# Reordering the transfers that bring in batch 1 in a fused FFT and gated-FFN kernel: row copies regrouped, the rows' load issued ahead of the table copies, the folds from step 19

## The chip, the cores and the metric

The kernel runs on one core of one Trainium2 chip. The metric is the device time of one execution in microseconds, the median of several runs. All times within an execution count from the start of its span, the first instruction of the program.

## What is computed

The reference takes x (8 batches of 3008 rows by 256 features), does a Fourier transform over rows and features and keeps the real part, and sends the 24064 rows that result through a gated feed-forward block:

```python
X = np.fft.fft(x, axis=1)
X = np.fft.fft(X, axis=2)
x = X.real.astype(np.float32).reshape(B * S, D)
gate = 1.0 / (1.0 + np.exp(-(x @ w_gate)))
val = x @ w_val
return (gate * val @ w_out).astype(np.float32)
```

w_gate and w_val are 256 by 1536, w_out is 1536 by 256.

## The kernel before, in words

The feature transform is merged into the gate and value weights when these are loaded (tiles G1, G2 and ge), the row transform is a set of matmuls against tables of cosines and sines, and the symmetry of both is used by folding: rows and features are added to and subtracted from their mirror images before the transform. Everything is float32.

**Steps.** The body is one loop (L1136 on) over steps i = 0, 1, 2, ...; a step handles one block of 128 hidden features of a chunk of up to 252 spectrum rows. There are 12 steps to a chunk (i0 = NFT = 12), three to a group p, six chunks to a batch (per = 72), 576 steps in all. In step i PE does the two halves of the gate and value product (`front_a`, pf<-pk; `front_b`, pf<-qk), and between them a third of the output product of group (i−5)//3 (`back`). ACT starts the next step's accumulator (`seed`, L766: ek times ge), makes copies and sigmoids; DVE forms z and h for step i−1 (L796, L808, L812). From the second chunk on the output product uses 15 products of sums instead of more plain ones: POOL makes these sums (`H_SUMS`, L818, tile sf), seven in steps with i % 3 = 2 and six in steps with i % 3 = 0. PE reads the first two of the six three steps later.

**Lists of side work.** What else has to be done is hung on the steps by hand: `at(i, f)` appends f to step i's list `side`, run at the step's end; `spare` and `gap` hold pieces for ACT and DVE within the step. A piece hung earlier in the code runs earlier in the step. The instructions of each engine run in the order in which this program issues them, and all transfers named below are issued by SP, in order. SP issues a transfer only when the eighth transfer before it has landed (transfers share eight semaphores in turn).

**The weights' stage** (steps 0 to 12). Weights come in pieces (L375), are converted on ACT, DVE and POOL (L382 to L397), and a merge in steps 1 to 8 (`merge`, up to L420) makes 256 columns of G1 and G2 on PE and ACT and issues two transfers of 128 four-byte values into ge (L420). The seeds of steps 6, 8 and 10, made one step ahead, read the ge values that are loaded in steps 4, 6 and 8: the load of the row that the change's title calls the G row's.

**Batch 1.** Batches after 0 go through a DRAM copy with rearranged rows, `xr`:

- `quarter_x(1)` gives 23 copies into xr: three of zeros (L155, L157), two of 128x3x256 (L168) and 18 of 4x32x256 or 4x31x256 (L163), all called row copies here.
- `load_x(1)` (L146) loads xr into the tile x4 in two halves of 1.5 MB. It needs all row copies landed and the weights' use of the same tile ended.
- `fold_ops(1, 2)` gives 24 pieces: two of L496 and six of L492 on POOL, six of L505 (five on DVE, one on POOL), three of L499 to L502, four of L531, three more of L499 to L502 on POOL. `first_folds` (hung on step 16) hangs them on the steps in `slots`.
- `table_rows` (L206) copies six parts of the cosine and sine tables, reversed, into the DRAM tile rtab, 2x32x753 each. `quarter_load` (L247), four calls of four transfers, loads the tables from the input and from rtab into SBUF.
- `quarter_small` (L255, L256, on ACT) picks columns from these tables, `quarter_other` (L262) moves them between partitions, and `ratios` (L272 to L281, on DVE) computes factors from them. Later POOL, DVE and ACT build smaller tables (`quarter_ops`, L292 to L318).
- `e_load(b)` (L683) loads one feature of every row of batch b into x8, seven transfers of 4-byte pieces; POOL folds x8 (`e_fold`, L687 to L690) in step 36.

The stores of a finished chunk (L921, L925) are issued by SP when DVE has transposed it (L912, tile os). The first chunk's 16 stores come in steps 16 and 17.

Of the kernel before, what the change touches and what calls it, by code (L numbers as in the profile page):

```python
# [81 lines left out]
def kernel(  # L82
# [60 lines left out]
    def load_x(b):  # L143
        X[b] = xp.tile([P, 4, NQ, D], F32, name="x4", tag="x4")
        for h in range(0, 4, 2) if b else ():
            nc.sync.dma_start(out=X[b][:, h : h + 2], in_=XR[b][:, h : h + 2])  # L146
# [3 lines left out]
    def quarter_x(b):  # L150

        copy = nc.sync.dma_start
        src = xf[b]
        dst = XR[b] = dram.tile([P, 4, NQ, D], F32, name=f"xr{b}")
        ops = [lambda: copy(out=dst[TB : TB + 1, :, N3], in_=zero[0:1].to_broadcast([1, 4, D]))]  # L155
        for q in (1, 1 + N3):
            ops.append(lambda q=q: copy(out=dst[HP - 1 : HP, :, q], in_=zero[0:1].to_broadcast([1, 4, D])))  # L157

        def run(lo, q, t, step, skip=0, less=0):
            n = TB - skip - less  # L160
            p0 = t // NQ + step * skip
            rows = src[p0 : p0 + n] if step > 0 else src[p0 - n + 1 : p0 + 1]
            copy(out=dst[lo + skip : lo + skip + n, :, q].rearrange("p h d -> h p d"),  # L163
                 in_=rows[:, :, t % NQ].rearrange("p h d -> h p d")[:, ::step])

        for par in range(2):
            lo = par * HP
            ops.append(lambda par=par, lo=lo: copy(out=dst[lo : lo + TB, :, 0:N3], in_=src[0:TB, :, par:NQ:2]))  # L168
            for q in range(N3):
                own = 2 * q + par  # L170
                less = int((par, q) == (0, 1))
                first = int((par, q) == (0, 0))
                ops += [lambda a=a: run(*a) for a in (
                    (lo, N3 + q, M // 2 - own, -1), (lo + TB, q, M // 4 - own, -1, 0, less),
                    (lo + TB, N3 + q, M // 4 + own, 1, first, less))]
        return ops
# [26 lines left out]
    def table_rows(par, q):  # L203

        p0, qq = divmod(M // 4 - 2 * q - par, NQ)
        nc.sync.dma_start(  # L206
            out=rtab[par * TB : (par + 1) * TB, :, q].rearrange("p t k -> t p k"),
            in_=stab[p0 - TB + 1 : p0 + 1, :, qq].rearrange("p t k -> t p k")[:, ::-1])
# [29 lines left out]
    def quarter_src(g, par, t, cols):  # L238
        return (stab[0:TB, t, par:NQ:2, cols], rtab[par * TB : (par + 1) * TB, t, :, cols])[g]

    def quarter_load(t, par):


        for name, cols in (("odd", slice(NE, NE + NO)), ("ev", slice(0, NE))):
            for g, own, lo in TILES:
                if own == par:
                    nc.sync.dma_start(out=TAB[name][lo : lo + TB, t ^ g, :, 0 : cols.stop - cols.start],  # L247
                                      in_=quarter_src(g, par, t, cols))

    def quarter_small(which, part):  # L250

        for g, par, lo in TILES:
            at_ = slice(lo, lo + TB)
            if (g, par) == (which, part):
                nc.scalar.copy(TAB["self"][at_, 0:N3], TAB["ev"][at_, g, :, 0])  # L255
                nc.scalar.copy(TAB["angle"][at_].rearrange("p (t q) -> p t q", t=2),  # L256
                               TAB["odd"][at_, :, :, 0] if g == 0 else TAB["odd"][at_, ::-1, :, 0])
# [6 lines left out]
    def small_ops():  # L264

        vec, sign = nc.vector, TAB["sign"]

        def signs():
            for g, par, lo in TILES:
                nc.gpsimd.memset(sign[lo : lo + TB], (1.0, -1.0)[g])  # L270
        return signs, (
            lambda: vec.reciprocal(TAB["less"], TAB["cos"]),  # L272
            lambda: vec.tensor_tensor(TAB["tan"], TAB["sin"], TAB["less"], op=ALU.mult),
            lambda: vec.tensor_scalar(out=TAB["less"], in0=TAB["tan"], scalar1=-1.0, scalar2=None, op0=ALU.mult),
            lambda: vec.reciprocal(TAB["self"], TAB["self"]),
            lambda: vec.tensor_tensor(TAB["other"], TAB["other"], TAB["self"], op=ALU.mult),
            lambda: vec.tensor_scalar(out=TAB["other"], in0=TAB["other"], scalar1=sign, scalar2=None, op0=ALU.mult),
            lambda: vec.reciprocal(TAB["cy"], TAB["ev"][:, 0, :, 1]),
            lambda: vec.tensor_tensor(TAB["cx"], TAB["ev"][:, 1, :, 1], TAB["cy"], op=ALU.mult),
            lambda: vec.tensor_scalar(out=TAB["cx"], in0=TAB["cx"], scalar1=sign, scalar2=None, op0=ALU.mult),  # L280
            lambda: vec.tensor_scalar(out=TAB["cy"], in0=TAB["cx"], scalar1=-1.0, scalar2=None, op0=ALU.mult))  # L281
# [400 lines left out]
    def e_load(b):  # L682
        nc.sync.dma_start(out=x8[:, b - 1], in_=xf[b, :, :, :, HD : HD + 1])  # L683
# [319 lines left out]
    side, mid, gap, spare = {}, {}, {}, {}  # L1003

    def at(i, *fs):
        side.setdefault(i, []).extend(fs)
# [18 lines left out]
    i0 = NFT  # L1025
    count = 3 * len(groups)
    calm = lambda lo: (i for i in range(lo, count) if 3 <= i % i0 <= 7)
    for i, f in enumerate(quarter_x(1)):
        at(1 + i // 2 if i < 16 else 9 + (i - 16) // 4, f)
    at(i0 + 1, lambda: load_x(1))  # L1030
    for b in range(1, B):
        at(18 + b, lambda b=b: e_load(b))
    at(3 * i0, e_fold)
    later_e = []
    at(3 * i0 + 4, lambda: later_e.extend(e_joint()))
# [5 lines left out]
        at(i - (8 if i == i0 else 11), lambda i=i: e_rows(i))  # L1041

    for i in range(NQ):
        at(11 + i // 3, lambda i=i: table_rows(i % 2, i // 2))
    at(i0 + 1, raw_tables)
    for i in range(4):
        at(14 + i // 2, lambda i=i: quarter_load(i // 2, i % 2))
    signs, ratios = small_ops()
    at(i0, signs)
    for i in range(4):  # L1050
        spare.setdefault(27 + i, []).append(lambda i=i: quarter_small(i // 2, i % 2))
    at(31, quarter_other)
    for i, f in zip((32, 33, 34, 42, 43, 44, 30, 31, 51, 52), ratios, strict=True):
        gap.setdefault(i, []).append(f)

    def first_folds():

        slots = [17, 17, 17, 18, 19, 20, 21, 22, 23, 24, 25, 25, 26, 26, 28, 30, 33, 35, 37, 39, 41, 44, 47, 50]
        for i, f in zip(slots, fold_ops(1, 2), strict=True):
            at(i, f)  # L1060
        for i, f in enumerate(TURN.pop(1)):
            gap[35 + i] = [f]
        swaps, last, first = MORE.pop(1)
        at(41, swaps[1])
        at(52, swaps[0])
        for i, f in enumerate(first):
            gap.setdefault(45 + i, []).append(f)
        for i, f in enumerate(last):
            gap[56 + i] = [f]

    def first_ends():
        one, two = quarter_ends(1, 1), quarter_ends(1, 0)
        for i, f in zip((55, 65, 65, 66, 66, 67, 67, 68, 68, 69, 69, 70, 70, 71, 71, 72, 73, 74, 75, 76),
                        one[0] + two[0] + one[1] + two[1], strict=True):
            gap.setdefault(i, []).append(f)
    at(16, first_folds)
    at(3 * i0 + 14, lambda: seq_start(1))
    for blk in range(2):
# [152 lines left out]
```

## Time and profile before

| what | value |
|---|---|
| median of 3 runs | 1927.27 us (1927.20 to 1927.51) |
| the profiled execution | 1926.32 us, span 1924.5 us |
| granted TensorE clock, mean | 0.997 |
| busy in the span: PE, DVE, ACT, POOL | 1900.8, 1520.1, 1351.8, 1542.9 us |
| L818 sums on POOL | 2392 instructions, 0.55 to 0.60 us each in the mean |
| L492 on POOL | 42 instructions, 1.27 us each |

How to read it: busy time of PE includes the pipelining of matmuls and is close to the span, so it is the gaps that are of interest. The waits say which engine stood for whom; the timeline gives for each instruction its start, duration and the idle time before it with what ended it; the windows give busy time of every engine, the granted clock and the DMA engines' share in a stretch; the chain of waits follows the work that ended last back through what released each step. Of SP the timeline shows how long it took to issue a transfer, not how long the transfer took.

### The profile page before, as it was taken

The numbers are of one execution on the slowest core, as the hardware profiler recorded it, in microseconds if no ns is written. First come the engines' busy times: TensorE is split into PE (matmuls) and PEld (weight loads), VectorE is DVE, ScalarE is ACT, GpSimd is POOL, SyncE is SP. The second block draws the span as 40 slices with busy tenths as digits, with TensorE's granted clock in tenths as the row PEclk, the third lists the DMA queues.
The fourth block names the chain that finished last, engine by engine and source line by source line (L and its number), as shares of the span: only waits on it lengthen the run. The fifth ranks groups of instructions, "written<-read, shape, count | busy, mean of one in ns | idle before, by whom it ended". The sixth has DMA issues, their size and how long they took to land.

```text
span 1924.5 us, 36049 instructions
## 1 busy us (share of the span) xinstructions
PE 1900.8 (99%) x11836; PEld 1758.3 (91%) x11836; DVE 1520.1 (79%) x3368; ACT 1351.8 (70%) x3235; POOL 1542.9 (80%) x2733
## 2 busy tenths in 40 slices
PE   8989999999999999999999999999999999999999
PEld 6669899999999999999999999999999999999998
DVE  7658879887988789797788877888788887976775
ACT  4757777676767677777777777777767777777775
POOL 2359969996999879997799977998789986877770
PEclk9989999999999999999999999999999999999999
DMA  8453231121112120221212112112120120010001
GB/s 312 124 152 19 63 115 54 52 64 56 39 45 71 40 80 19 61 58 31 85 32 62 40 36 88 39 47 48 35 80 14 30 45 15 15 22 20 14 17 30
DMA packets 196661, 109.33 MB, mean 57 GB/s; under 512 B 134791, under 2 KB 187762, under 8 KB 194682
## 3 DMA queue, kind: packets, MB, share of 16 engines
q1 hardware_dynamic: 195896, 106.50, 20.7%
q8 instruction: 95, 1.56, 0.4%
q14 instruction: 92, 0.75, 0.1%
q10 hardware_dynamic: 546, 0.51, 0.1%
q0 software_dynamic: 32, 0.00, 0.0%
HBM read 71.24 MB, written 47.87 MB: 62 GB/s over the span
## 4 chain that ended last, share of the span: by engine, by line
PE 87%; POOL 5%; DMA 3%; DVE 2%; ACT 2%; issue 1%; SPq 0%; POOLq 0%; ACTq 0%; DVEq 0%
PE pf L133 46%; PE po L133 38%; POOL sf L818 3%; PE sum L133 2%; DMA x<-xr 1%; POOL x L492 1%; DMA x<-in_xf_dram 1%; DMA ge<-G 1%; DVE c L902 1%; DVE z L796 0%; POOL x L505 0%; PE ps L133 0%; ACT pf L766 0%; DMA raw<-in_moe_w_val_dram 0%; DVE h L812 0%
## 5 line engine op out<-in xcount | busy, mean ns | idle before, releaser
L818 POOL TENSOR_TENSOR sf<-h,sf 128x168 f32<-128x168 f32 (+1 forms) x1104 | 619.5, 581 | 77.8 <-DVE h L812 75.4
L818 POOL TENSOR_TENSOR sf<-h 128x168 f32<-128x168 f32 (+1 forms) x920 | 520.7, 585 | 160.5 <-DVE h L812 159.4
L133 PE MATMUL pf<-qk,G 128*128 128x252 f32 (+1 forms) x2304 | 584.7, 376 | 1.7 <-ACT ae L781 1.5
L133 PE MATMUL pf<-pk,G 128*128 128x252 f32 (+1 forms) x2304 | 583.3, 376 | 2.3 <-ACT pf L766 2.3
L766 ACT ACTIVATE pf<-ek,ge 128x252 f32<-128x252 f32 (+1 forms) x1142 | 538.2, 471 | 27.0 <-DMA ge<-G 7.1
L133 PE MATMUL po<-sf,wf 128*128 128x168 f32 (+1 forms) x2944 | 509.4, 306 | 9.9 <-POOL sf L818 9.9
L781 ACT ACTIVATE ae<-pf 128x504 f32<-128x504 f32 (+1 forms) x576 | 338.8, 588 | 213.2 <-PE pf L133 211.8
L133 PEld LDWEIGHTS pf<-pk,G 128*128 128x128 f32 x2304 | 435.8, 190 | 56.8 <-ACT pf L766 4.3
L133 PEld LDWEIGHTS po<-sf,wf 128*128 128x128 f32 x2944 | 453.8, 190 | 18.6 <-POOL sf L818 10.6
L133 PE MATMUL po<-h,wf 128*128 128x168 f32 (+2 forms) x2584 | 461.2, 307 | 0.0
L812 DVE TENSOR_TENSOR h<-pf,z 128x252 f32<-128x252 f32 (+1 forms) x576 | 240.4, 417 | 279.6 <-ACT pf L809 275.9
L796 DVE TENSOR_TENSOR z<-ae,pf 128x504 f32<-128x504 f32 (+1 forms) x576 | 384.6, 668 | 92.6 <-ACT h L795 89.0
L902 DVE TENSOR_TENSOR c<-c 128x168 f32<-128x168 f32 (+1 forms) x920 | 442.9, 505 | 3.3
L133 PEld LDWEIGHTS pf<-qk,G 128*128 128x128 f32 x2304 | 410.9, 190 | 34.1 <-ACT ae L781 4.2
L133 PEld LDWEIGHTS po<-h,wf 128*128 128x128 f32 x2584 | 410.3, 190 | 17.6 <-issue 0.9
L795 ACT ACTIVATE h<-pf 128x252 f32<-128x252 f32 (+1 forms) x576 | 216.8, 376 | 156.5 <-PE pf L133 140.0
L809 ACT ACTIVATE pf<-z 128x252 f32<-128x252 f32 (+1 forms) x576 | 214.3, 372 | 124.1 <-DVE h L808 122.3
L808 DVE TENSOR_TENSOR h<-h,pf 128x252 f32<-128x252 f32 (+1 forms) x576 | 232.8, 404 | 0.0
L818 POOL TENSOR_TENSOR sf<-sf 128x168 f32<-128x168 f32 (+1 forms) x184 | 101.9, 554 | 14.4
L818 POOL TENSOR_TENSOR sf<-sf,h 128x168 f32<-128x168 f32 (+1 forms) x184 | 109.6, 595 | 0.0
L885 ACT COPY c<-po 128x504 f32<-128x504 f32 (+1 forms) x138 | 78.5, 569 | 0.4 <-PE po L133 0.3
L912 DVE STREAM_TRANSPOSE os<-c 128x256 f32<-128x256 f32 x188 | 76.5, 427 | 0.4 <-issue 0.3
(151 smaller groups left out, 874.2 us busy)
## 6 DMA issues: line engine op xcount, KB each, us to landing
x<-xr SPq DMA_DIRECT2D x14, 1536.0 KB
out_dram<-os SPq DMA_DIRECT2D x376, 56.0 KB
xr<-in_xf_dram SPq DMA_DIRECT2D x105, 128.0 KB
x<-x SPq DMA_DIRECT2D x112, 96.0 KB
xr<-in_xf_dram SPq DMA_DIRECT2D x14, 384.0 KB
ek<-ed SPq DMA_DIRECT2D x40, 126.0 KB
out_dram<-os SPq DMA_DIRECT2D x288, 7.0 KB
x<-in_xf_dram SPq DMA_DIRECT2D x3, 1024.0 KB
```

Of the source, the lines that this page charges most:

```text
L133: nc.tensor.matmul(o, l, r, start=start, stop=stop, skip_group_check=True)
L766: nc.scalar.activation(PF[i][:, g], EK[i // NFT], AF.Copy, scale=ge[:, g, f : f + 1])
L781: nc.scalar.activation(AP[i], PF[i], AF.Copy, scale=2.0)
L795: nc.scalar.activation(H[p][:, fh, 0:n], PF[i][:, 0], AF.Sigmoid)
L796: nc.vector.tensor_tensor(z[:, :, ::-1], AP.pop(i), PF[i], op=ALU.subtract)
L808: nc.vector.tensor_tensor(h[:, fh, 0:n], h[:, fh, 0:n], pf[:, 1], op=ALU.mult)
L809: nc.scalar.activation(pf[:, 0], z[:, 0], AF.Sigmoid)
L812: nc.vector.tensor_tensor(h[:, fh, n:], pf[:, 0], z[:, 1], op=ALU.mult)
L818: nc.gpsimd.tensor_tensor(block(p, dst), block(p, a), block(p, b), op=(ALU.subtract, ALU.add)[op])
L885: (nc.vector.tensor_copy if t == 1 or t == 3 else nc.scalar.copy)(C[0][:, 3 * t * R : 3 * (t + 1) * R], PO[t][:, 0 : 3 * R])
L902: nc.vector.tensor_tensor(t[:, dst * R : (dst + 1) * R], *v, op=(ALU.subtract, ALU.add)[op])
L912: nc.vector.transpose(os_[0][0][:, s, 0:nb, h, :], t[:, c0 : c0 + nb * TB])
```

## The change

Only the steps on which pieces are hung change; no piece is added, removed or altered.

- Row copies: of the 20 pieces 3 to 22 some move by a step. Steps 1 to 8 had two copies each; now odd steps have one and even steps three. Steps 9 and 10 keep four and three.
- The table copies (L206) go from steps 11 and 12 to steps 14 and 15, so the x load (step 13) and the load of ek of the same step are issued ahead of them.
- The table loads (L247) go from steps 14 and 15 to 17 and 18, which puts them behind the first chunk's 16 stores.
- The seven loads of x8 (L683) go from steps 19 to 25 to steps 21 to 27, `quarter_small` from 27 to 30 to 29 to 32, `quarter_other` from 31 to 33, three of the ratios a step on.
- The folds of batch 1 begin in step 19 instead of 17; from the seventeenth piece on (step 33) they stay where they were.

```diff
-    for i, f in enumerate(quarter_x(1)):
-        at(1 + i // 2 if i < 16 else 9 + (i - 16) // 4, f)
+    for i, f in zip((1, 2, 2, 2, 3, 4, 4, 4, 5, 6, 6, 6, 7, 8, 8, 8, 9, 9, 9, 9, 10, 10, 10), quarter_x(1), strict=True):
+        at(i, f)
     at(i0 + 1, lambda: load_x(1))
     for b in range(1, B):
-        at(18 + b, lambda b=b: e_load(b))
+        at(20 + b, lambda b=b: e_load(b))
...
     for i in range(NQ):
-        at(11 + i // 3, lambda i=i: table_rows(i % 2, i // 2))
+        at(14 + i // 3, lambda i=i: table_rows(i % 2, i // 2))
     at(i0 + 1, raw_tables)
     for i in range(4):
-        at(14 + i // 2, lambda i=i: quarter_load(i // 2, i % 2))
+        at(17 + i // 2, lambda i=i: quarter_load(i // 2, i % 2))
     signs, ratios = small_ops()
     at(i0, signs)
     for i in range(4):
-        spare.setdefault(27 + i, []).append(lambda i=i: quarter_small(i // 2, i % 2))
-    at(31, quarter_other)
-    for i, f in zip((32, 33, 34, 42, 43, 44, 30, 31, 51, 52), ratios, strict=True):
+        spare.setdefault(29 + i, []).append(lambda i=i: quarter_small(i // 2, i % 2))
+    at(33, quarter_other)
+    for i, f in zip((33, 33, 34, 42, 43, 44, 31, 32, 51, 52), ratios, strict=True):
         gap.setdefault(i, []).append(f)
...
     def first_folds():
-        slots = [17, 17, 17, 18, 19, 20, 21, 22, 23, 24, 25, 25, 26, 26, 28, 30, 33, 35, 37, 39, 41, 44, 47, 50]
+        slots = [19, 19, 19, 20, 20, 21, 22, 23, 24, 25, 26, 26, 27, 27, 29, 31, 33, 35, 37, 39, 41, 44, 47, 50]
         for i, f in zip(slots, fold_ops(1, 2), strict=True):
             at(i, f)
```

## The prediction

> **What bounds the kernel now.** The page first: PE is busy 1900.8 of 1924.5 us, so the kernel can gain only where PE stands still or is slowed, 23.7 us in all. The chain of waits over 100 to 160 us tells where most of that is.
>
> ```profile
> 104.62 20.17 DMA x<-xr
> 125.13 3.54 issue
> 130.12 2.48 POOL sf L818 x5
> 133.22 2.44 POOL x L492 x2
> ```
>
> The path waits 20.17 us for the load of batch 1's rows (L146), then runs through POOL. The timelines of POOL and PE (start, duration, instruction, idle time before it and what ended it) show the order:
>
> ```profile
> 113.39 0.53 POOL L818 TENSOR_TENSOR sf<-h 128x168 f32<-128x168 f32 x1
> 124.92 0.21 POOL L496 TENSOR_TENSOR x<-x 128x6 f32<-128x6 f32 x1 [11.00 <-DMA x<-xr]
> 128.70 0.21 POOL L496 TENSOR_TENSOR x<-x 128x6 f32<-128x6 f32 x1 [3.57 <-DMA x<-xr]
> 130.67 1.49 PE L133 MATMUL po<-sf,wf 128*128 128x168 f32 x4 [9.06 <-POOL sf L818]
> ```
>
> POOL meets the first fold at 113.9 and stands 14.6 us for the two halves of the load. Step 18's sums (L818) are queued behind the folds, step 21's products need them, and PE stops for 9.06 us. Steps counted by their first pf<-pk matmuls on PE: an undisturbed step takes 3.125 us, step 21 takes 13.89 (119.74 to 133.63). The granted clock is 1.00 before and 0.63 from 121.5 to 130.7, so the matmuls after the gap run slowly too: step 22 takes 3.40. POOL then works without a pause to 220 us with a backlog; step 27 waits for it (4.48).
>
> Why the load is late stands in SP's queue and in the DMA share by windows (the last two numbers are the share of 16 engines and GB/s):
>
> ```profile
> 80.39 9.50 SPq L163 DMA_DIRECT2D xr<-in_xf_dram  x9
> 89.93 14.51 SPq L206 DMA_DIRECT2D rtab<-in_stab_dram  x6
> 104.62 4.97 SPq L146 DMA_DIRECT2D x<-xr  x2
> 84.00:96.00 12.00, 12.00 (x42) 7.73 (x41) 8.43 (x17) 10.22 (x27) 6.56 (x10) 1.00 0.27 97
> 96.00:109.00 13.00, 13.00 (x52) 9.35 (x51) 9.73 (x24) 9.89 (x29) 8.63 (x20) 1.00 0.14 52
> 109.00:117.00 8.00, 8.00 (x47) 7.53 (x46) 6.88 (x18) 6.02 (x17) 2.90 (x5) 1.00 0.98 368
> ```
>
> One engine is a share of 0.06. The row copies (L163) keep about four engines busy until their last one lands at 96.43; the six table copies (L206) keep two busy, 4 us each, to 120.15. The x load, 3 MB, needs 11 us where nothing lies ahead of it (batch 2's is issued at 281.25 and its halves land at 288.84 and 292.51). Here it is issued at 104.62 behind the table copies: fourteen engines end near 117, the two others begin their part at about 119 and land the halves at 124.78 and 128.63.
>
> The second place is the weights' stage. ACT's timeline has the seeds (L766) waiting for the loads of ge (L420):
>
> ```profile
> 72.70 0.47 ACT L766 ACTIVATE pf<-ek,ge 128x252 f32<-128x252 f32 x1 [4.11 <-DMA ge<-G]
> 82.73 0.47 ACT L766 ACTIVATE pf<-ek,ge 128x252 f32<-128x252 f32 x1 [2.28 <-DMA ge<-G]
> ```
>
> They lengthen step 7 to 6.64 (5.12 without: steps 5 and 6) and step 9 to 4.81 (3.39 without: steps 12 to 14).
>
> **The change, part by part.** No instruction is added or removed.
>
> *The x load ahead of the table copies, folds from step 19.* The load needs the row copies (96.43) and the weights' tile (POOL's last join ends at 93.4), so it issues near 96.5 and lands at about 104 and 108. POOL reaches the first fold after step 18's sums. With step 17 at 106.0 (below), step 18 begins at 109.2, its sums become ready 3.45 us into it (3.41 in steps 54 and 57, 3.78 in step 17) and six of 0.55 end at 115.9. The load is there 8 us earlier: the wait goes, and step 18's sums stand ahead of the folds anyway. What goes with it is 13.89 − 3.125 = 10.77 in step 21, 0.28 in step 22 and, if POOL keeps up, 4.48 − 3.125 = 1.36 in step 27: **12.4 us**.
>
> *Does POOL keep up?* Six point folds (L492, 1.27) lie in steps 19 to 23 among 13 sums per three steps. At 0.55 a sum (0.54 to 0.55 is the median of the four kinds at 250 to 400 us; their mean over the kernel is 0.58) POOL is through step 19 at 117.6, step 20 at 124.2, step 21 at 128.8 (its first two sums at 125.3), step 23 at 135.2, step 24's first two sums at 136.3. Step 24's products want 125.3 by about 129.6, step 27's want 136.3 by 139.0. Margins 4.3 and 2.7, so I count no wait. Twenty sums lie between 117.6 and 136.3, so a sum of 0.68 uses the margin up. The last fold on POOL (L505, 1.28, now in step 27) ends near 147, with step 30's sums done at 143.5. The five L505 on DVE (0.69) each stand a step later, before the chunk's L902 sums start in step 28: no cost.
>
> The row on contention: points took 1.26 to 1.27 at 129 to 146 while DVE was busy 26% to 72%, and 1.260 / 1.270 / 1.417 us (least, median, most) over all 42. The Trainium skill, "SBUF — State Buffer", section "Who interferes with whom", says that a DVE instruction with two SBUF inputs and a GpSimd instruction that reads SBUF exclude each other for a whole instruction. By it the folds, which ran while DVE waited, would now be held up by z, h and c products of 0.4 to 0.7 us; the spread of 1.260 to 1.417 bears out little of that for points, more for the sums (0.53 at least, 0.9 at most). It is the first rival below.
>
> *Step 48.* ACT waited 2.03 us at 220.86 for POOL's L295, at the end of POOL's backlog, and step 48 took 4.63 (+1.5). POOL's work from 128.7 to 220.84, 92.1 us, less step 18's sums (3.1) now begins at 115.9 and can end at 205, or at 207 with 2 us of waits for h. Step 47 began 55.5 after step 30 and ACT came to the wait 3.0 into it: 146.6 + 58.5 = 205.2 here. The wait is nothing to 1.8 us, so nothing to 1.5 is gained; I take the middle, **0.7**.
>
> *Row copies bunched.* Step 6's urgent ge load still has the copies of steps 4 and 5 ahead of it since 60 us, four in both kernels (two and two before, three and one now) on four engines that have no pause between 62 and 72.6: no gain in step 7, bounds 0 and one copy's 1.37 us. For step 8's load (78.53, landed 82.65) the 128x3x256 copy (L168; 384 packets of 0.05 us over 16 engines, 1.2 us) moves behind it. PE stood 0.97 us there. Gain 0 to 1.2; I take **1.0**. The ge loads of odd steps get one copy more ahead of them (1.37 us on four engines: step 7's lands at 78 instead of 76.9) and are read at 80. So step 17 begins at 107.24 less 1.0 to 1.2; I reckon with 106.0, and a shift of it moves both sides of every margin. The last copies stay bound by the four engines: 96.4.
>
> *What moves behind.* The table copies start after the load, at 107.7, and land every 4 us to 131.7 (to 120.15 before). The 16 stores of the first chunk now come ahead of the 16 table loads (L247). SP issues a transfer only when the eighth before it has landed: a table load waited 4.3 us for the x load on that account at 124.80. So the eighth store waits for the last table copy, 131.7; the rest takes 8 × 0.45 (stores at 135.07 to 142.36), and the table loads run from 135.3 at 0.53 (12 from 128.65 to 134.97). ACT's copies L255 want the ninth load in step 29: issued at 139.5, landed 4.9 later (as the one of 128.65, which landed at 133.55) at 144.4, wanted at 143.5 + 2.5 = 146.0 (2.5 from step 27). The slack is 1.6 us, and 2.5 in step 30: no cost, but thin cover. The Trainium skill, "DMA: Bandwidth & Descriptors", section "Why a DMA increments its semaphore by 16 and not by 1", has a transfer over k engines use the lowest-numbered k. Stores would then share the table copies' two engines and land behind them; were it otherwise, the table loads would wait for the last table copy alone and the slack would be some 3 us more. The seven x8 loads (2.0 each) then end near 160, before POOL's L687 near 172. Ratios, small<-small and the rest move by a step or two and are wanted ten steps later.
>
> *Sum.* 12.4 + 1.0 + 0.7 = 14.1. The profiled execution took 1926.32 (span 1924.5 and 1.8 around it), so 1912.2. The median of the runs is 0.95 above it: **1913.2**. PE is the bound from 243 us on at 3.05 to 3.125 a step, so nothing takes it back.
>
> **The rivals.**
>
> *POOL becomes the bound* (0.12). For: POOL is busy 9.8 of 10 us from 130 to 230 and more folds now fall on fewer steps. Against: 14.6 us of idle time are back, and at 300 to 360 us POOL is as full with no PE gap. Price: at 0.75 a sum step 27 waits 1.4, and step 48's gain goes too: 14.1 − 2.1 leaves 12, 1915.3; 1918 if step 24 waits as well.
>
> *The load still comes late* (0.04): SP held somewhere else, the load landing as before at 128.6. Then only the two steps count: folds 1.7, step 20's sums 3.9, points 2.5 and two sums 1.1 end at 137.8, where step 24 wants 129.6; 8 us stay and 1921 comes out.
>
> *Tables late* (0.14, of which 0.04 slower). ACT blocks at L255 in step 29 and every sigmoid stands behind it. For: the table loads have moved behind 24 us of copies on two engines and behind 16 stores. Against: 1.6 us of slack by rows that were themselves taken behind a backlog. One us of further delay costs one us: 5 us late gives 1916.6. Slower than before begins 1.6 + 14.1 = 15.7 us late; from the ninth store to the ninth load lie two rounds of eight transfers, each of which would have to take 8 us more than the 4 that the rows give. With 20 us late it is 1931.6.
>
> **How the numbers follow.** Forecast 0.70 (1910 to 1916 by itself: less step 7's 1.4 and step 48's 0.8 more, or none of the two small gains). The range reaches down to these and up to the POOL rival and a mild table wait: 1909.5 to 1918.5. Faster by over 0.2% (3.9 us, about what a measurement here can tell from no change): 0.70 + 0.12 + 0.04 + 0.07 = 0.93; within 0.2% 0.03; slower 0.04.
>
> **What would show it.** Right: x<-xr issued before rtab near 96.5; no wait of POOL for it; no PE gap near 120 and a granted clock of 1.00 there; step 21 at 3.1; L766's 2.28 shrunk to about 1, the 4.11 unchanged. Wrong: an idle stretch of PE before po in steps 24 or 27 ended by POOL L818, or of ACT before L255 ended by st<-rtab or st<-in_stab; or L295 holding ACT longer than 2 us.

## The result and the profile after

The changed kernel took **1910.93 us** (median of 4 runs, 1910.83 to 1912.48), the kernel before 1927.39 beside it (4 runs, 1927.20 to 1929.22): a ratio of 0.9914, 95% interval 0.9897 to 0.9932. The profiled execution took 1910.83 with a span of 1909.0, against 1926.32 and 1924.5: 15.5 us less. The forecast of 1913.2 was 2.3 too high and its range held the time.

First the chain of waits of the changed kernel from 60 us on (start, length, what); in the kernel before it had 20.17 us of the x load at 104.62:

```profile
67.14 3.87 DMA ge<-G
...
76.93 3.33 DMA ge<-G
...
113.57 1.70 PE pf L133 x8
115.27 1.43 PE po L133 x10
116.70 1.70 PE pf L133 x8
118.40 1.43 PE po L133 x10
```

From 82 us on it holds nothing but PE's own matmuls; what is left of waiting are the two loads of ge. The timeline of SP, then of POOL, and the windows (busy us of PE, PEld, DVE, ACT, POOL; granted clock, DMA share, GB/s):

```profile
79.45 9.98 SPq L163 DMA_DIRECT2D xr<-in_xf_dram  x9
96.27 0.82 SPq L146 DMA_DIRECT2D x<-xr  x2
97.14 0.42 SPq L754 DMA_DIRECT2D ek<-ed  x1
97.60 17.57 SPq L206 DMA_DIRECT2D rtab<-in_stab_dram  x6
115.28 3.65 SPq L921 DMA_DIRECT2D out_dram<-os  x1
```

```profile
114.82 0.67 POOL L818 TENSOR_TENSOR sf<-sf 128x168 f32<-128x168 f32 x1
115.46 0.47 POOL L496 TENSOR_TENSOR x<-x 128x6 f32<-128x6 f32 x2
115.89 1.26 POOL L492 TENSOR_TENSOR x<-x 128x510 f32<-128x510 f32 x1
117.12 2.45 POOL L818 TENSOR_TENSOR sf<-h 128x168 f32<-128x168 f32 x4
```

```profile
96.00:109.00 13.00, 13.00 (x55) 9.79 (x54) 10.17 (x26) 9.50 (x25) 7.57 (x16) 1.00 0.71 263
109.00:117.00 8.00, 8.00 (x50) 7.59 (x49) 6.87 (x16) 6.65 (x18) 7.39 (x14) 1.00 0.13 49
121.50:130.70 9.20, 9.20 (x55) 8.46 (x54) 6.88 (x12) 6.23 (x15) 9.12 (x13) 1.00 0.21 65
```

The x load is issued at 96.27, takes the first stretch (share 0.71; 0.14 before), and its halves land at 102.61 and 106.68 by the records of its semaphore. The table copies have the second stretch to themselves (0.13 is two engines of 16). POOL comes to L496 at 115.46 and stands for nothing. In the third stretch PE is busy throughout at a granted clock of 1.00. The same stretch of the kernel before, with 0.14 of 9.20 us and 0.63:

```profile
121.50:130.70 9.20, 0.14 (x2) 0.03 (x1) 1.02 (x4) 1.02 (x3) 2.21 (x5) 0.63 0.29 91
```

Where the 15.5 us come from, by steps (beginnings of PE's pf<-pk groups in both traces):

| steps | before, us | after, us | saved |
|---|---|---|---|
| 7, 8 | 6.64, 5.22 | 5.12, 5.12 | 1.62 |
| 9 | 4.81 | 3.94 | 0.87 |
| 21, 22, 27 | 13.89, 3.40, 4.48 | 3.12, 3.12, 3.12 | 12.4 |
| 23 | 3.12 | 3.25 | −0.13 |
| 48 | 4.63 | 3.69 | 0.94 |

The rest of the kernel gives 0.2 us back.

### The profile page after: what moved, and what is told of

Its sections match the earlier page's. It is cut to its first block, busy times and chain, and to the rows that moved or that the text cites. A ratio compares the mean times of both kernels' runs of the same rounds, so it can differ in the third digit from the quotient of the medians.

```text
span 1909.0 us, 36050 instructions
## 1 busy us (share of the span) xinstructions
PE 1897.8 (99%) x11836; PEld 1756.7 (92%) x11836; DVE 1525.7 (80%) x3368; ACT 1353.5 (71%) x3235; POOL 1546.6 (81%) x2733
## 4 chain that ended last, share of the span: by engine, by line
PE 93%; POOL 2%; DVE 2%; ACT 2%; DMA 2%; issue 0%; SPq 0%; ACTq 0%; POOLq 0%
PE pf L133 49%; PE po L133 41%; PE sum L133 2%; POOL sf L818 1%; DMA x<-in_xf_dram 1%; DMA ge<-G 0%; PE ps L133 0%; DVE c L902 0%; ACT pf L766 0%; DMA raw<-in_moe_w_val_dram 0%; ACT pf L809 0%; DVE z L796 0%; PE ev L133 0%; PE od L133 0%; ACT ae L781 0%
## 5 line engine op out<-in xcount | busy, mean ns | idle before, releaser
L818 POOL TENSOR_TENSOR sf<-h,sf 128x168 f32<-128x168 f32 (+1 forms) x1104 | 620.8, 582 | 76.2 <-DVE h L812 74.2
L818 POOL TENSOR_TENSOR sf<-h 128x168 f32<-128x168 f32 (+1 forms) x920 | 522.7, 587 | 159.9 <-DVE h L812 158.8
L766 ACT ACTIVATE pf<-ek,ge 128x252 f32<-128x252 f32 (+1 forms) x1142 | 538.4, 471 | 24.5 <-DMA ge<-G 4.3
L781 ACT ACTIVATE ae<-pf 128x504 f32<-128x504 f32 (+1 forms) x576 | 339.3, 589 | 210.9 <-PE pf L133 209.0
L902 DVE TENSOR_TENSOR c<-c 128x168 f32<-128x168 f32 (+1 forms) x920 | 447.7, 510 | 3.3
L796 DVE TENSOR_TENSOR z<-ae,pf 128x504 f32<-128x504 f32 (+1 forms) x576 | 384.9, 668 | 79.8 <-ACT h L795 76.2
L809 ACT ACTIVATE pf<-z 128x252 f32<-128x252 f32 (+1 forms) x576 | 214.6, 373 | 128.3 <-DVE h L808 125.8
L808 DVE TENSOR_TENSOR h<-h,pf 128x252 f32<-128x252 f32 (+1 forms) x576 | 233.2, 405 | 0.0
L818 POOL TENSOR_TENSOR sf<-sf 128x168 f32<-128x168 f32 (+1 forms) x184 | 102.2, 555 | 14.4
L818 POOL TENSOR_TENSOR sf<-sf,h 128x168 f32<-128x168 f32 (+1 forms) x184 | 109.9, 597 | 0.0
```

What stands on the lines that cost most here:

```text
L766: nc.scalar.activation(PF[i][:, g], EK[i // NFT], AF.Copy, scale=ge[:, g, f : f + 1])
L781: nc.scalar.activation(AP[i], PF[i], AF.Copy, scale=2.0)
L796: nc.vector.tensor_tensor(z[:, :, ::-1], AP.pop(i), PF[i], op=ALU.subtract)
L808: nc.vector.tensor_tensor(h[:, fh, 0:n], h[:, fh, 0:n], pf[:, 1], op=ALU.mult)
L809: nc.scalar.activation(pf[:, 0], z[:, 0], AF.Sigmoid)
L818: nc.gpsimd.tensor_tensor(block(p, dst), block(p, a), block(p, b), op=(ALU.subtract, ALU.add)[op])
```

## Experiments

Each kernel was timed beside the kernel before, which took 1926.1 to 1926.4 there. The changed kernel once more, to compare with:

> The changed kernel once more, unaltered, on the same chip as the three that follow, so that these can be set against it: 1910.9 us, within 0.9 of it, and 0.9914 of the kernel before. Theory and rival alike.

Measured: 1910.75 (1910.24 to 1912.15), ratio 0.992 [0.9906, 0.9933]. Steps 7 to 9 took 14.02 us together (14.17 in the first profile), all later steps the same within 0.1.

**The parts one by one.** The row copies alone, in the kernel before:

```diff
-    for i, f in enumerate(quarter_x(1)):
-        at(1 + i // 2 if i < 16 else 9 + (i - 16) // 4, f)
+    for i, f in zip((1, 2, 2, 2, 3, 4, 4, 4, 5, 6, 6, 6, 7, 8, 8, 8, 9, 9, 9, 9, 10, 10, 10), quarter_x(1), strict=True):
+        at(i, f)
```

> The kernel before with the row copies regrouped and nothing else changed. Theory (the x load is the bound, and it comes late because of the table copies on two engines): the weights' stage gets about 2.4 us shorter (steps 7 and 9), but the row copies still end near 96.4 on their four engines and the load still lands near 124.7 and 128.6, so PE's gap in step 21 grows by the same 2.4 us: 1927.3 us, within 0.6. Rival (the gain of the regrouping stands by itself): 1925.

Measured: 1926.03 (1925.44 to 1927.50), ratio 0.9999 [0.999, 1.0008]. The waits of this kernel between 100 and 145 us (total, times, longest) and its SP timeline say where the gain went:

```profile
POOL x L496 <- DMA x<-xr: 16.8, 2, 13.3
...
PE po L133 <- POOL sf L818: 11.3, 1, 11.3
```

```profile
89.58 14.77 SPq L206 DMA_DIRECT2D rtab<-in_stab_dram  x6
104.53 4.64 SPq L146 DMA_DIRECT2D x<-xr  x2
```

Steps 7 to 9 fell from 16.68 to 14.32 us, as in the changed kernel. But the x load went out at 104.53 (104.62 before), behind copies whose pace does not depend on PE; POOL came 2.3 us earlier and stood 16.8 instead of 14.6, and step 21 took 16.10 instead of 13.89. A gain upstream of a fixed arrival is waited away. The expected 1927.3 was reckoned from the 1927.27 that the kernel before had taken earlier; beside the 1926.38 measured here it is the ratio that counts, and it says no change, as the theory did, where the rival's 1925 would be 0.9988.

The changed kernel with the old distribution of row copies (the same lines the other way):

> The changed kernel with the row copies of steps 1 to 8 as before (two a step). Theory: the stall at step 21 is gone by the order of load and table copies alone, and the 2.4 us of the weights' stage are lost again, because with the load early they count in full: 1913.3 us, with waits of 4.1 and 2.3 us at L766. Rival (the regrouping matters little once the load is early): 1911.

Measured: 1912.39 (1912.07 to 1914.12), ratio 0.9931 [0.9918, 0.9945]: halfway between theory and rival. The waits at L766 were 3.24 and 2.29 us, not 4.1 and 2.3. With the load out of the way the regrouping is worth 1.6 us by the medians, though the two ratios' intervals overlap (0.9906 to 0.9933 for the changed kernel). Steps 7 to 9 took 15.82; over all profiles they took 15.8 to 17.0 with the old distribution (3 kernels), 13.9 to 15.3 with the new one (7 kernels). The size of this gain thus differs from execution to execution by about as much as the gain itself.

The later folds alone, in the kernel before, and the old fold slots in the changed kernel:

```diff
-        slots = [17, 17, 17, 18, 19, 20, 21, 22, 23, 24, 25, 25, 26, 26, 28, 30, 33, 35, 37, 39, 41, 44, 47, 50]
+        slots = [19, 19, 19, 20, 20, 21, 22, 23, 24, 25, 26, 26, 27, 27, 29, 31, 33, 35, 37, 39, 41, 44, 47, 50]
```

> The kernel before with only the folds moved to the new steps; the load stays behind the table copies and lands near 124.7 and 128.6. Theory: step 18's sums get ahead of the waiting folds, PE passes step 21 and stands in step 24 instead, for about 6.3 us, and 1 us in step 27; with the slow clock after it 8 us are lost instead of 12.4: 1923 us (1921.5 to 1925). Rival (POOL's wait costs the same wherever it stands): 1927.

Measured: 1923.20 (1922.36 to 1924.85), ratio 0.9984 [0.9975, 0.9993]. POOL's wait fell to 10.7 us; step 21 took 3.12, but steps 23, 24, 25 and 27 took 4.12, 9.84, 3.46 and 3.86, 8.8 us too long: the wait moved three steps on, to the next sums behind the folds. As the theory had it.

> The changed kernel with the folds in the steps of before (from step 17). Theory: the load lands near 104 and 107, POOL comes to the first fold near 111.5, so there is no wait for it; POOL does its points two steps sooner and has its backlog sooner behind it: 1910.9 us, within 0.7, L295 holding ACT no longer than 1.1 us. Rival (the shift of the folds is a needed part): points ahead of step 18's sums make PE wait in steps 21 to 27, 1912 to 1915.

Measured: 1912.45 (1912.13 to 1913.58), ratio 0.993 [0.9918, 0.9943]: the rival's time, but by another way. POOL waited for no load here either, yet steps 20, 21 and 23 took 3.60, 3.29 and 3.81, 1.20 us more than those three in the changed kernel. (This profile has two more differences that the folds' place need not have made: 0.7 us in steps 7 to 9, and 1.15 in steps 101 and 102, of which more below.) The timelines of POOL (first) and DVE of this kernel show what happened:

```profile
112.44 1.26 POOL L492 TENSOR_TENSOR x<-x 128x510 f32<-128x510 f32 x1
...
117.15 2.59 POOL L492 TENSOR_TENSOR x<-x 128x510 f32<-128x510 f32 x2
```

```profile
112.46 1.53 DVE L453 TENSOR_TENSOR wf<-wc 128x256 f32<-128x256 f32 x1
...
116.72 1.90 DVE L456 TENSOR_TENSOR wf<-wf,wc 128x128 f32<-128x128 f32 x2
118.54 0.67 DVE L796 TENSOR_TENSOR z<-ae,pf 128x504 f32<-128x504 f32 x1
```

L453 and L456 are DVE's one-time sums of output weights, with both inputs in SBUF. The form of L453 that reads wc alone takes 0.40 us and L456 0.28 where POOL runs short sums. Started just after a fold, L453 ends 0.29 us after the fold's end (113.99, 113.70); the second L456 (1.35 by itself, to 118.62) ends 0.2 after the first of the next two folds (117.15 and 1.27). z and h (L796, L808) stand behind them on DVE, ACT's L809 waits for L808 (1.25 us at 115.49) with ae (L781) behind it, and PE waits for ae. To tell this from "POOL's sums come late behind the folds", each point fold of batch 1 was cut in two:

```diff
-            e.tensor_tensor(x4[:, i, q, 1:D], x4[:, i, q, 1:D], x4[:, j, q, D - 1 : 0 : -1],
-                            op=ALU.add)
+            for k in range(q.start, q.stop) if b == 1 else (q,):
+                e.tensor_tensor(x4[:, i, k, 1:D], x4[:, i, k, 1:D], x4[:, j, k, D - 1 : 0 : -1],
+                                op=ALU.add)
```

> The run with the old fold slots (from step 17) was 1.5 us over the changed kernel though POOL waited for no load; its steps 20, 21 and 23 took 3.60, 3.29 and 3.81, and DVE's weight sums took up to 1.53 us (L453) and 1.35 us (L456) where 0.40 and 0.28 are usual, beside point folds of 1.27 us on POOL. Here the same slots, with each point fold of batch 1 cut in two instructions of 255 elements a partition. Theory (a DVE sum with two SBUF inputs stands until POOL's running fold ends): the longest L453 and L456 fall to about 0.9-1.0, the excess of the three steps from 1.33 us to 0.7 or less, the time by 0.3 to 1 us. Rival (POOL's sums come late because the folds stand ahead of them): POOL's work is the same or 0.4 us longer, so nothing falls, and the time is that of the uncut run or 0.3 more.

Measured: 1911.86 (1909.36 to 1913.21), ratio 0.9923 [0.9911, 0.9936]; the time alone decides nothing. The steps do: 20, 21 and 23 took 3.23, 3.15 and 3.12. DVE's timeline of this kernel at the same place (its lines behind the cut count one more, so z is L797):

```profile
112.87 0.98 DVE L453 TENSOR_TENSOR wf<-wc 128x256 f32<-128x256 f32 x1
...
117.11 0.82 DVE L456 TENSOR_TENSOR wf<-wf,wc 128x128 f32<-128x128 f32 x2
117.86 0.67 DVE L797 TENSOR_TENSOR z<-ae,pf 128x504 f32<-128x504 f32 x1
```

The hold-up halves with POOL's instruction (1.53 to 0.98, 1.90 to 0.82), though POOL's folds together became longer. By the rival none of this should have fallen, so it is excluded. The time shows less of it because steps 7 to 9 took 15.34 in this profile.

**How early must the load be?** Four of the six table copies put ahead of the x load again (with `i < 2` in place of `i < 4`, two):

```diff
-        at(14 + i // 3, lambda i=i: table_rows(i % 2, i // 2))
+        at(12 if i < 4 else 14, lambda i=i: table_rows(i % 2, i // 2))
```

> The size of the main effect: the changed kernel with four of the six table copies issued ahead of the x load again, two behind it. Theory (the load's halves land behind the copies on two engines, 4 us later for each; POOL is ready at 115.5 and its backlog has margins of 4.3 us in step 24 and 2.7 in step 27): halves land at about 116.8 and 120.6, POOL stands about 1.3 and 3.5 us before L496, and the margins do not hold: steps 24, 25, 27 and 48 wait 0.9, 0.2, 2.4 and 0.6 more by the ledger of POOL's work, 4.1 us in all, 1915 (1913.5 to 1916.5). Rival (any wait of POOL for the load ends at PE in full): 4.8 us and more, or none at all if the copies' engines matter less than the order on SP.

> The same with two table copies ahead of the x load and four behind it. Theory: the halves land at about 108.8 and 112.6, POOL is ready at 115.5 and waits for neither, no step between 20 and 27 grows: the time of the changed kernel, 1910.8 within 0.9. Rival (the load's earliness itself is worth something, or the copies slow it further than 4 us each): POOL waits in step 19, 1912 to 1915.

| copies ahead | halves land, us | POOL waits, us | longer than 3.125 in steps 20 to 30 | median, us |
|---|---|---|---|---|
| 0 (changed kernel again) | 103.71, 107.53 | 0 | 0.14 | 1910.75 |
| 2 | 107.83, 111.55 | 0 | 0.13 | 1910.91 |
| 4 | 115.64, 119.34 | 3.3 | 1.98, in step 27 | 1915.10 |
| 6 (later folds alone, old row copies) | 125.17, 129.01 | 10.7 | 8.8 | 1923.20 |

Ratios: two copies 0.9922 [0.9909, 0.9936], four 0.9942 [0.9928, 0.9955]. A copy ahead delays the load by 2.0 to 4.8 us, by the differences between these rows (3.9 from two to four copies), and nothing is lost until POOL is ready at 115.5. Behind four copies the wait comes out at PE by less than itself, and not at once. PE's timeline of that kernel, then ACT's:

```profile
137.76 0.45 PE L133 MATMUL po<-h,wf 128*128 128x168 f32 x2
139.70 1.05 PE L133 MATMUL po<-sf,wf 128*128 128x168 f32 x4 [1.49 <-POOL sf L818]
```

```profile
208.56 0.68 ACT L318 ACTIVATE st<-st 128x570 f32<-128x570 f32 x1 [2.60 <-POOL st L295]
```

Step 24 had margin enough (0.9 was expected there), step 27 lost 1.98 (2.4 expected) and step 48 1.25 more than in the changed kernel (0.6): 3.2 us in the steps of which the theory spoke, for its 4.1. That the medians differ by 4.4 is in part chance: 1.15 us of this profile's difference lies in steps 101 and 102, where one DVE instruction took long. Its row in this kernel, then in the changed one:

```profile
380.18 2.27 DVE L550 SCALAR_TENSOR_TENSOR x<-x,small 128x256 f32<-128x256 f32 x1 [1.12 <-DMA out_dram<-os]
...
377.11 0.80 DVE L550 SCALAR_TENSOR_TENSOR x<-x,small 128x256 f32<-128x256 f32 x1 [1.11 <-DMA out_dram<-os]
```

It stood beside a row of POOL's L531 and L818 whose first gap is at 382.18, and ended 0.27 us after that. The run with folds from step 17 had the same (2.22 us, the same 1.15 in the same steps), though its load was early; in the 12 other profiles this L550 took 0.98 at most and step 102 took 3.12. In the changed kernel it ran beside such a row as well, so what makes the difference stays open.

**What delays the ge load of step 6.**

```diff
-    for i, f in zip((1, 2, 2, 2, 3, 4, 4, 4, 5, 6, 6, 6, 7, 8, 8, 8, 9, 9, 9, 9, 10, 10, 10), quarter_x(1), strict=True):
+    for i, f in zip((1, 2, 2, 2, 3, 4, 4, 5, 6, 6, 6, 7, 8, 8, 8, 8, 9, 9, 9, 9, 10, 10, 10), quarter_x(1), strict=True):
```

> Disputed: what delays the ge load of step 6 (L766 waits 2.24 us for it in step 7). The changed kernel with one of step 4's three row copies put behind that load, so that three copies instead of four stand ahead of it. Rival (the prediction's reckoning: the four engines run without a pause from 62 us, so each copy ahead costs its 1.37 us): the wait falls to about 0.9 and step 7 to about 3.9-4.1, the kernel gains up to 1.3 us, less what the fourth copy in step 8 takes. Theory (the weights' transfer issued at 64 moves slowly on the same engines while all 16 are in use, and a copy ahead of it only fills that time): the wait stays near 2.2, step 7 near 5.1, and the time within 0.5 us of the changed kernel.

Measured: 1910.27 (1910.09 to 1911.07), ratio 0.9917 [0.9903, 0.993]; the wait in step 7 was 2.53, not 0.9. The semaphore records give the landing on the last four engines, those with the row copies (weights L375 issued near 64, copies of step 5 behind it, then ge issued near 67):

| kernel | weights landed, last engine | copies after them | last copy landed | ge landed on the four |
|---|---|---|---|---|
| before | 69.56 | 2 | 72.32 | 71.06, 71.55, 72.08, 72.61 |
| after | 69.51 | 1 | 70.83 | 70.62, 70.67, 70.94, 71.01 |
| this one | 69.45 | 1 | 70.82 | 69.53, 69.86, 69.93, 71.00 |
| early copies (below) | 68.28 | 0 | – | 68.91, 68.94, 68.95, 68.98 |

With three copies ahead of the weights' load (after) or two (before, this one) its last share landed at 69.5 in these profiles. Over all profiles it landed at 68.70 to 69.56 with two ahead (4 profiles) and at 69.41 to 69.96 with three (8): the third copy ahead costs some 0.5 us in the mean, while each copy behind it adds 1.3 to 1.4 us on the slowest engine. The wait stayed, as the theory had it. But three of the four engines did gain about a microsecond from the missing copy, as the rival had it, and the load is complete only with the fourth, so this one profile does not settle the theory's reason. Why that one engine's share was late is not shown.

**No row copies in steps 5 and 7**, with and without halved folds:

```diff
-    for i, f in zip((1, 2, 2, 2, 3, 4, 4, 4, 5, 6, 6, 6, 7, 8, 8, 8, 9, 9, 9, 9, 10, 10, 10), quarter_x(1), strict=True):
+    for i, f in zip((1, 1, 1, 2, 3, 3, 3, 4, 4, 6, 6, 6, 6, 8, 8, 8, 9, 9, 9, 9, 10, 10, 10), quarter_x(1), strict=True):
```

> The changed kernel with no row copy in steps 5 and 7, three in step 1, one in step 2, three in step 3, two in step 4, four in step 6, three in step 8. By both accounts fewer copies stand ahead of the ge load of step 6, so its wait in step 7 falls from 2.24 to about 0.9 and the one in step 9 from 1.40 to about 0; step 7 about 4, step 9 about 3.4. Theory: this carries to the end, as in the run with the old copies, 1.0 to 1.8 us faster than the changed kernel, if the earlier copies do not hold the weights of steps 1 to 4 (each copy more ahead of such a load 1.37 us on four engines). Rival: steps 2 to 6 grow by as much, and the time is that of the changed kernel or up to 1 us more.

Measured: 1910.24 (1909.84 to 1911.83), ratio 0.9919 [0.9905, 0.9932]. The waits fell to 0.44 and 0.81, step 9 to 3.39. But step 7 stayed at 5.12, the length of its merge, not 4: a wait of 2.2 us there already lay beside other work. What is gained is step 9's 0.3 to 0.6 us, too little for the times to tell from the changed kernel. So the theory's 1.0 to 1.8 us did not come, and not for the rival's reason either, since steps 2 to 6 did not grow.

> The changed kernel with the early row copies (none in steps 5 and 7) and the point folds of batch 1 cut in halves: the fastest version that the runs point to. Theory (both small gains stand, 0.5 to 0.9 us from the copies and about 0.13 us from step 23's hold-up of DVE): 1909.4 to 1910.4, no L453 or L456 over 1.0 us, step 23 at 3.12. Rival (each half costs POOL a fixed part more, 3 pairs more of work while POOL has a backlog, so step 24, 27 or 48 waits): 1910.5 to 1912.

Measured: 1910.55 (1910.40 to 1912.56), ratio 0.9922 [0.9908, 0.9935]. Both theory and rival were at work: by step 23 this kernel was 0.84 us ahead of the changed one, with no L453 or L456 over 0.81, and step 48 gave 0.93 back. Its ACT timeline there:

```profile
205.35 0.68 ACT L318 ACTIVATE st<-st 128x570 f32<-128x570 f32 x1 [2.03 <-POOL st L295]
```

Halved folds cost POOL 1.41 us a pair instead of 1.26, six pairs 0.9 us, and by as much L295, at the end of POOL's backlog, came later. None of the versions is measurably faster than the changed kernel.

**The cover of the table loads.**

```diff
-        spare.setdefault(29 + i, []).append(lambda i=i: quarter_small(i // 2, i % 2))
+        spare.setdefault(27 + i, []).append(lambda i=i: quarter_small(i // 2, i % 2))
```

> What the later picks protect: the changed kernel with ACT's copies from the tables (L255, L256) back in steps 27 to 30. In the changed kernel the table load that the first of them needs lands at 142.22 us and ACT's seeds of step 27 end at 138.8, those of step 29 at 144.95. Theory (the slack of the picks is 2.8 us in step 29 and so is used up in step 27): ACT stands 3.4 us before L255 in step 27, every ae (L781) behind it is late, PE stands 2.5 to 3.4 us, and the time is 1913 to 1914.5. Rival (ACT has time to spare and PE work queued): the wait is there, but the time stays within 0.8 us of the changed kernel's 1910.8.

Measured: 1914.50 (1914.10 to 1915.77), ratio 0.9941 [0.9928, 0.9953]: the theory. ACT's timeline, then PE's:

```profile
139.56 0.18 ACT L255 COPY small<-st 32x3 f32<-32x3 f32 x1
142.86 0.20 ACT L256 COPY small<-st 32x6 f32<-32x6 f32 x1 [3.11 <-DMA st<-in_stab_dram]
...
144.01 0.56 ACT L781 ACTIVATE ae<-pf 128x504 f32<-128x504 f32 x1
```

```profile
144.63 1.12 PE L133 MATMUL pf<-qk,G 128*128 128x252 f32 x4 [1.95 <-ACT ae L781]
```

It is L256, the copy after L255, that wants the ninth load (landed 142.83 here). ACT stood 3.11 us, steps 28 and 30 grew by 2.65 together; another 0.83 of this profile's difference lies in steps 7 to 9.

## Why the prediction was right, and where it failed

**The load ahead of the copies: right.** Predicted 12.4 us in steps 21, 22 and 27, measured 12.4. The load was issued at 96.27 (near 96.5 predicted) and was there 1.3 us earlier than reckoned. The clock's part came along: 1.00 where 0.63 was granted. The new order of load and copies was not run without the other two parts; the runs with old row copies and with old folds, each some 14 us faster than the kernel before, show that it carries most of the gain.

**POOL keeps up: right.** Folds began at 115.46 (115.9 predicted). Behind four copies POOL began the first point fold 3.7 us later (119.57) and PE met the sums 1.7 us late (139.70 instead of 138.04, where the products of h end): a margin of 2.0 in step 27, predicted 2.7. The rival "POOL becomes the bound" did not occur, but it begins with two microseconds of lost POOL time. The rival of a late load reckoned with 8 us that stay; with the later folds alone it was 8.8.

**Contention: looked for on the wrong engine.** The prediction asked whether POOL's folds would be held up by DVE and found little in their durations. The six folds did keep their length (1.26 to 1.32 us); it was DVE that stood. Nor was it z or h, which the prediction had named: they read one input from pf, which lies in PSUM, and z kept its 0.67 us beside the second of the two folds of the trace above (118.54). The instructions that stood, L453 and L456, have both inputs in SBUF. In the changed kernel that costs 0.13 us (step 23), with folds from step 17 1.2 us. So the later folds had a use that the prediction did not give them: with the load early they were not needed for the load at all, but they come mostly behind DVE's weight sums. The Trainium skill, "SBUF — State Buffer", section "Who interferes with whom", has a DVE instruction with two SBUF inputs contend with a GpSimd instruction that reads SBUF, calls the shared port pair an exclusive lock, and lets the order of issue decide who blocks. The first DVE trace above agrees: L453, started 0.02 us after the fold, took 1.53 us where 0.40 is usual.

**Step 48: right in mechanism, near in size.** 0.94 for 0.7, where the 0.7 was the middle of 0 to 1.5; ACT's wait fell from 2.03 to 1.14, inside the predicted 0 to 1.8:

```profile
205.28 0.68 ACT L318 ACTIVATE st<-st 128x570 f32<-128x570 f32 x1 [1.14 <-POOL st L295]
```

**Step 7: this is the step that failed.** "No gain in step 7", because four copies stand ahead of the ge load in both kernels "on four engines that have no pause between 62 and 72.6", bounds 0 and 1.37. Measured 1.52, and ACT's timeline shows the wait, predicted unchanged at 4.11, at 2.24:

```profile
71.10 0.47 ACT L766 ACTIVATE pf<-ek,ge 128x252 f32<-128x252 f32 x1 [2.24 <-DMA ge<-G]
...
80.35 0.47 ACT L766 ACTIVATE pf<-ek,ge 128x252 f32<-128x252 f32 x1 [1.40 <-DMA ge<-G]
```

Counting copies was wrong because the weights' load stands between them: in these two profiles its last share landed at 69.5 whether two or three copies were ahead of it, so the copy that went from behind it to ahead of it cost nothing there and was saved behind. By the landings in order, the weights' share took 1.9 to 2.4 us on the four engines behind the ge load ahead of it in the kernel before, and 1.0 in the changed one: the four engines were busy, but not at a fixed pace, and "no pause" in a share by windows does not say that. What sets the pace stays open. The size has luck in it: with the old distribution step 7 took 6.64, 6.20 and 5.77 in three kernels, with the new one 5.12 to 5.34, and the prediction started from the longest. These 1.52 us are the 1.4 by which the sum of 14.1 fell short of 15.5; the other differences nearly cancel. The remaining 0.9 of the forecast's 2.3 is the allowance of 0.95 between the profiled execution and the median, which came out at 0.1 (1910.83 and 1910.93).

**Step 9: right** (0.87 for 1.0; its wait 2.28 became 1.40), with a spread from 3.67 to 4.77 for the same order of copies that no single profile shows.

**Tables: right.** The last table copy landed about 130.6 (131.7), the ninth load at 142.22 (144.4), wanted at 145.0 (146.0). The slack is 2.8 us instead of 1.6, and the run with the earlier picks shows its end: two steps earlier ACT stands.

## What to carry to other kernels

When an engine waits for a transfer, look at what stands ahead of that transfer on its queue and on the few engines it shares, and order the queue by when each result is needed; beyond the consumer's own readiness earliness is worth nothing (two copies ahead cost nothing, four cost 3.2 us in the steps that waited). A gain ahead of a fixed arrival shows no time until the arrival is moved too, so parts that measure as nothing alone may count together. Before moving long instructions of one engine, look at what the engine that shares its ports has to do in the new place, and at the duration of *its* instructions.

## What the runs showed of the hardware

A sum of 0.40 us on DVE with both inputs in SBUF took 1.53 us beside a POOL instruction of 1.26, and 0.98 beside halves of it. One scalar-tensor-tensor instruction of DVE (L550) took 2.27 and 2.22 us beside POOL sums in two profiles and 0.98 at most in the 12 others. A transfer that spreads over 16 engines lands with the slowest of them: the x load's share on the two engines with table copies landed 8.5 to 9.2 us after its other shares behind four copies (114.91 and 115.64; 106.44). Steps 7 to 9, whose length hangs on loads of four-byte pieces behind row copies, varied by 1.4 us over profiles of the same order of copies.
